# Attention and MLP on one core: the third group's values right behind its denominators, two turns a burst sooner, four second-MLP pieces in the first period

## The chip, the cores and the metric

The kernel runs on one core of one Trainium2 chip. The metric is the time of an execution in microseconds (us), in medians. Ratios are the mean time of one kernel's fast runs over the mean of the other's fast runs of the same rounds, so they are not quite the ratio of the medians quoted beside them. "Faster" or "slower" needs 2%, here 9 us; smaller differences are read from the ratio's 95% interval.

## The reference

```python
q, k, v: (8 batches, 12 heads, 448, 64);  g_q, g_k: (64,)
q_n, k_n = q / rms(q) * g_q, k / rms(k) * g_k
attn = softmax(q_n @ k_n.T / 8);  x = (attn @ v), heads side by side: (3584, 768)
h = x @ w_in                       # 768 x 2048
g = max(h, 0) + alpha * min(h, 0)
out = g @ w_out                    # 2048 x 768
```

## The kernel before

A batch's 12 heads are worked on in three groups of 4 heads, so there are 24 groups, numbered 0 to 23. A group has 7 score tiles. The program is a list of 66 bursts; a burst holds two or three score tiles and their exponentials, sometimes a group's denominators (`den`) or values (`attv`), and, from the end of batch 0 on, pieces of the MLP: up-projections (`up`, x times w_in, one of 16 tiles of the hidden layer) and second-MLP pieces (`down`, times w_out). Between a batch's last `attv` and the next batch's lies a period, whose bursts share out 16 `up` and some `down`.

The scheduling is by hand: every engine runs its instructions in the order in which this program emits them.

```python
    pss = ... "pss", bufs=2, PSUM      # score tiles, 2 banks each
    psa = ... "psa", bufs=1, PSUM      # one accumulator of 2 banks: den, attv, turns, spare
    psf = ... "psf", bufs=2, PSUM      # two of 1 bank: up, down, early turns, spin
    ...
    def square(y, nm):   # y >= 2: GpSimd
    def reduce(y, nm):   # VectorE: sums of squares
    def root(y):         # ScalarE: Ln, Exp
    def scale(y, nm):    # VectorE for q of groups 1 to 3, GpSimd for their k; then GpSimd for both
    def turn(y):         # TensorE transposes, VectorE writes qT and kT (k with its gain)
    ...
    # plan of the bursts
        if len(dens) > len(avs):
            avs[n] = len(avs)
        elif len(dens) < NG and last_in.get(len(dens), n) < n:
            dens[n] = len(dens)
    ...
    turn_at[2] = av_at[0] + 1
    for y in range(G, NG):
        early = y < G + 2
        n = turn_at[y - 1] if early else max(d for d in dens if d <= turn_at[y] - 2)
        at(n - (8 if early else 5), load_qk, y)
        for nm in "qk":
            (after if early else at)(n - 2, square, y, nm)
            if early:
                after(n, reduce, y, nm)
    ...
        roots[n + 1] = y
    ...
        tail = len(new) if b == B - 1 else 2 if odd or b == 0 else 1
    ...
    # burst of group 2's denominators (lead), and the next
        if lead and n in dens:
            den(dens[n]); log(dens[n]); invert(dens[n])
        elif lead:
            attv(avs[n])
```

With one accumulator, group 2's values can only start when ScalarE's logarithm has read the denominators. `spin` is a dummy matmul; the program puts spins where TensorE has nothing else to run.

Of the kernel before, what the change touches and what calls it, by code (L numbers as in the profile page):

```python
# [9 lines left out]
FP32 = mybir.dt.float32  # L10
# [11 lines left out]
def kernel(  # L22
# [14 lines left out]
    B, H, S, D = q.shape  # L37
# [4 lines left out]
    G = HH // 2  # L42
# [6 lines left out]
    TD = min(8, NG)  # L49
# [5 lines left out]
    pss = ctx.enter_context(tc.tile_pool(name="pss", bufs=2, space=bass.MemoryType.PSUM))  # L55
    psa = ctx.enter_context(tc.tile_pool(name="psa", bufs=1, space=bass.MemoryType.PSUM))
# [118 lines left out]
    def turn(y):  # L175

        if y >= TD:
            t = qkT[y, "k"].rearrange("p j g c -> p (j g c)")
            nc.vector.tensor_scalar(
                out=t, in0=t, scalar1=gain[:, 0:1], scalar2=None, op0=ALU.mult  # L180
            )
            return
        if y < G:
            ps = [psf.tile([128, 512], FP32, name="tps", tag="mm") for _ in "qk"]
        else:
            ps2 = psa.tile([128, 2, 512], FP32, name="tps2", tag="acc")
            ps = [ps2[:, 0], ps2[:, 1]]
        tps = [
            t[:, : S].bitcast(FP16).rearrange("p (j c) -> p j c", j=J) for t in ps
        ]  # L190
        for tp, nm in zip(tps, "qk"):
            for j in range(J):
                nc.tensor.transpose(  # L193
                    tp[:, j, :], qs[y, nm][:, j].rearrange("p h d -> p (h d)"), ident
                )
        for tp, nm in zip(tps, "qk"):
            t = att.tile([128, J, 2, 64], FP16, name=f"{nm}T", tag=f"{nm}T", bufs=4)
            o = t.rearrange("p j g c -> p j (g c)")
            if nm == "q" and y == 0:
                nc.scalar.copy(out=o, in_=tp)  # L200
            elif nm == "q":
                nc.vector.tensor_copy(out=o, in_=tp)
            else:
                nc.vector.tensor_scalar(  # L204
                    out=o, in0=tp, scalar1=gain[:, 0:1], scalar2=None, op0=ALU.mult
                )
            qkT[y, nm] = t
# [23 lines left out]
            scale=QK_SCALE, bias=expb[:, 0:1],  # L231
        )

    def over_keys(name, y, weights):
        acc = psa.tile([128, 2, 512], FP32, name=name, tag="acc")
        e = expT[y]
        for j in range(J):
            for g in range(2):
                for par in range(2):
                    nc.tensor.matmul(  # L240
                        out=acc[ds(64 * par, 64), g, :S],
                        lhsT=weights(g, par, j),
                        rhs=e[ds(64 * g, 64), j, par, :],
                        start=(j == 0),
                        stop=(j == J - 1),
                    )
        return acc
# [5 lines left out]
    def log(y):  # L253
        r = att.tile([128, 2, S], FP32, name="rden", tag="rden")
        nc.scalar.activation(out=r, in_=rden[y][:, :, :S], func=AF.Ln)  # L255
        rden[y] = r

    def invert(y):
        r = rden[y]
        nc.scalar.activation(out=r, in_=r, func=AF.Exp, scale=-1.0)  # L260

    def attv(y):
        b, i = divmod(y, G)
        vv = vt[b]
        av = over_keys("av", y, lambda g, par, j: vv[ds(64 * g, 64), 2 * i + par, j, :])
        if i == 0:
            xT[b] = att.tile([128, 2, G, S], FP16, name="xT", tag="xT")
        nc.vector.tensor_mul(  # L268
            out=xT[b][:, :, i, :], in0=av[:, :, :S], in1=rden[y]
        )  # L270
# [52 lines left out]
    def spin(count):  # L323

        if count:
            ps = psf.tile([128, 512], FP32, name="spin", tag="mm")
            for _ in range(count):
                nc.tensor.matmul(
                    out=ps[:, :S], lhsT=ident, rhs=idle, start=True, stop=True
                )  # L330
# [6 lines left out]
    while m < NG * J or len(avs) < NG:  # L337
        n = len(bursts)
        if len(dens) > len(avs):
            avs[n] = len(avs)  # L340
        elif len(dens) < NG and last_in.get(len(dens), n) < n:
            dens[n] = len(dens)
        three = n in dens and dens[n] >= G or n in avs and avs[n] >= G
        count = min(3 if three else 2, NG * J - m)
        bursts.append([divmod(m + c, J) for c in range(count)])
        for y, j in bursts[n]:
            first_in.setdefault(y, n)
            if j == J - 1:
                last_in[y] = n
        m += count  # L350
# [11 lines left out]
    turn_at = {  # L362
        y: max(n for n in range(first_in[y]) if n not in dens) for y in range(1, NG)
    }
    turn_at[2] = av_at[0] + 1
    turns = {n: y for y, n in turn_at.items()}
    jobs = {}
    for y in range(G, NG):

        early = y < G + 2  # L370
        n = turn_at[y - 1] if early else max(d for d in dens if d <= turn_at[y] - 2)
        at(n - (8 if early else 5), load_qk, y)
        for nm in "qk":
            (after if early else at)(n - 2, square, y, nm)
            if early:
                after(n, reduce, y, nm)
            else:
                jobs.setdefault(n, []).append((reduce, (y, nm)))
        roots[n + 1] = y
# [7 lines left out]
    for b in range(B):  # L387
        ups = [(UP, up, (b, ft)) for ft in range(NF)]
        odd = b % 2
        new = [  # L390
            (DOWN, down, (b - odd, t, oh))
            for t in (range(3, J) if odd else range(3)) for oh in range(2)
        ]
        tail = len(new) if b == B - 1 else 2 if odd or b == 0 else 1
        periods.append((ups, carry, new[:tail]))
        carry = new[tail:]

# [91 lines left out]
    for n in range(NB):  # L489
        for f, a in prep.get(n, ()):  # L490
            f(*a)
        tiles = bursts[n]

        lead = n in (den_at[G - 1], av_at[G - 1])
        if lead and n in dens:
            den(dens[n])
            log(dens[n])
            invert(dens[n])
        elif lead:
            attv(avs[n])  # L500
        for t in tiles[:2]:
            score(*t)
        plain = n not in dens and n not in avs
        wait = plain and gaps[n] and gaps[n][0][0] is up
        if lead and n in avs:
            spin(3)
        for t in tiles[:1] if wait else tiles[:2]:
            soft(*t)
        if n in dens and not lead:
            den(dens[n])  # L510
        if n in avs and not lead:
            attv(avs[n])
        for t in tiles[2:]:
            score(*t)
            soft(*t)
        late = []
        if wait:
            late = [(1, soft, t) for t in tiles[1:]]
        if n in roots:
            y = roots[n]  # L520
            root(y)
            for nm in "qk":
                scale(y, nm)
            if y >= TD:
                turn_dma(y)
        if n in dens and not lead:
            log(dens[n])
            if gaps[n] and gaps[n][0][0] is down:
                invert(dens[n])
            else:  # L530
                late = [(1, invert, (dens[n],))]
        done = 0

        spare_at, clock = [], 0.0
        for k, (f, a) in enumerate(gaps[n][:-1]):
            free = 2.3 if n in dens else 1.2 if n in avs else 0.1
            if clock >= free and not turns.get(n, TD) < TD and (
                not spare_at or k - spare_at[-1] > 2
            ):
                spare_at.append(k)  # L540
            clock += DOWN if f is down else UP
        for k, (f, a) in enumerate(gaps[n]):
            spare = k in spare_at
            if f is down:
                down(*a, jobs.pop(n, ()), spare)
            else:
                f(*a, spare)
                done += 1
                if late and done == late[0][0]:
                    for _, g, c in late:  # L550
                        g(*c)
                    late = []
            if n in turns and k == (
                0 if turns[n] >= TD else max(min(1, len(gaps[n]) - 2), 0)
            ):
                turn(turns[n])
        if not gaps[n] and n in turns:
            turn(turns[n])
        for _, g, c in late:
            g(*c)  # L560
        if n < den_at[G - 1] - 1 and plain and n not in turns:
            spin(4)
        elif lead and n in dens:
            spin(8)
        for f, a in jobs.pop(n, []) + post.get(n, []):
            f(*a)
    for k, (f, a) in enumerate(rest):
# [31 lines left out]
```

## Time and profile before

| | before |
|---|---|
| median of 3 runs | 449.81 us (449.42 to 450.79) |
| span of the profile | 449.1 us |
| TensorE, ScalarE, VectorE, GpSimd busy | 95%, 65%, 46%, 38% |
| first up-projection | 46.92 us |

The prediction below shows the lines and how they are read.

### The profile page before, as it was taken

The page shows a single profiled execution, that of the slowest core. Times are in us where ns is not written, and L with a number is a line of the kernel's source. Part 1 is how long each engine was busy: PE and PEld are TensorE (multiplying, and loading weights), DVE is VectorE, ACT ScalarE, POOL GpSimd, SP SyncE. Part 2 cuts the span into 40 slices and gives each one's busy share as a digit, 9 for nine tenths or more (in the row PEclk, how much of TensorE's full clock was granted, in tenths as well). Part 3 has the DMA queues.
Part 4 walks back from the last instruction along what each step waited for, and adds up shares of the span by engine and source line. Part 5 has one row for each costly group of instructions (what it writes and reads, how often), then busy time and mean ns, then how long its engine had stood idle before and what let it go on. Part 6 is the DMA issues. An engine that isn't in the chain of part 4 may idle for free.

```text
span 449.1 us, 9101 instructions
## 1 busy us (share of the span) xinstructions
PE 426.1 (95%) x3844; PEld 230.2 (51%) x3844; DVE 207.9 (46%) x297; ACT 290.9 (65%) x401; POOL 171.3 (38%) x125
## 2 busy tenths in 40 slices
PE   6877889889999999999999999999999999999996
PEld 2344444555545555545555545545555545555563
DVE  2656454735454545445454545444553343243421
ACT  4899788578776768578675868568675857222300
POOL 4769954660671460760671460760642000000000
PEclk9699999999999999999999999999999999999999
DMA  8999997295656651773567651782353401111122
GB/s 183 231 234 241 234 241 148 27 186 127 136 102 143 160 118 41 121 180 80 136 103 176 159 125 37 124 184 72 77 92 82 77 2 37 36 35 36 35 72 70
DMA packets 60009, 52.77 MB, mean 118 GB/s; under 512 B 32688, under 2 KB 56512, under 8 KB 59968
## 3 DMA queue, kind: packets, MB, share of 16 engines
q1 hardware_dynamic: 47424, 39.27, 37.3%
q0 software_dynamic: 11808, 11.81, 16.9%
q10 hardware_dynamic: 736, 1.11, 1.1%
q8 instruction: 30, 0.49, 0.5%
q14 instruction: 11, 0.09, 0.1%
HBM read 45.62 MB, written 11.01 MB: 126 GB/s over the span
## 4 chain that ended last, share of the span: by engine, by line
PE 82%; ACT 10%; DVE 4%; DMA 1%; issue 1%; POOL 0%; SPq 0%; ACTq 0%
PE op L301 32%; PE hT L284 19%; PE hTa L284 10%; PE sc L217 8%; ACT expT L229 5%; PE dn L240 5%; PE av L240 5%; PE opa L301 2%; DMA nat<-in_k_dram 1%; ACT ah L292 1%; ACT rden L260 1%; PE tps L193 1%; ACT rden L255 1%; DVE gT L293 1%; DVE ss L141 1%
## 5 line engine op out<-in xcount | busy, mean ns | idle before, releaser
L229 ACT ACTIVATE expT<-sc,expb 128x896 f16<-128x896 f32 x168 | 158.3, 1008 | 20.0 <-PE sc L217 19.7
L301 PE MATMUL op<-w_out_sb,gT 128*128 128x384 f16 x848 | 145.4, 326 | 0.0
L158 POOL TENSOR_TENSOR qs<-nat,rr 128x896 f16<-128x896 f32 x44 | 78.4, 1800 | 175.5 <-issue 138.1
L301 PEld LDWEIGHTS <-gT 128*128 128x128 f16 x896 | 84.6, 98 | 62.5 <-issue 9.1
L284 PE MATMUL hT<-xT,w_in_sb 128*128 128x448 f16 x534 | 112.7, 353 | 1.4 <-DVE gT L293 1.4
L284 PEld LDWEIGHTS <-w_in_sb 128*128 128x128 f16 x768 | 73.8, 98 | 71.5 <-issue 6.8
L292 ACT ACTIVATE ah<-hT,cols 128x448 f16<-128x448 f32 x89 | 56.5, 635 | 64.2 <-PE hT L284 64.1
L293 DVE TENSOR_TENSOR gT<-hT,ah 128x448 f16<-128x448 f32 x89 | 55.6, 625 | 64.8 <-ACT ah L292 64.8
L135 POOL TENSOR_TENSOR sq<-nat 128x896 f32<-128x896 f32 x44 | 73.1, 1683 | 1.5 <-DVE kT L204 1.4
L313 DVE COPY osb<-op 128x384 f32<-128x384 f32 x53 | 29.6, 558 | 93.6 <-PE op L301 93.6
L217 PE MATMUL sc<-qT,kT 64*64 64x448 f16 x672 | 53.8, 364 | 9.8 <-ACT expT L229 5.1
L141 DVE TENSOR_REDUCE ss<-sq 128x14 f32<-128x896 f32 x48 | 49.9, 1077 | 6.7 <-ACT sq L133 6.5
L284 PE MATMUL hTa<-xT,w_in_sb 128*128 128x448 f16 x234 | 50.6, 352 | 0.0
L292 ACT ACTIVATE ah<-hTa,cols 128x448 f16<-128x448 f32 x39 | 24.7, 635 | 39.6 <-PE hTa L284 39.6
L293 DVE TENSOR_TENSOR gT<-hTa,ah 128x448 f16<-128x448 f32 x39 | 24.4, 625 | 34.5 <-ACT ah L292 34.5
L217 PEld LDWEIGHTS <-kT 64*64 64x64 f16 x672 | 19.1, 105 | 40.0 <-issue 28.0
L240 PE MATMUL av<-expT,vt 64*64 64x448 f16 x672 | 36.0, 350 | 2.2 <-ACT rden L255 2.2
L240 PE MATMUL dn<-expT,ones 64*64 64x448 f16 x672 | 35.9, 349 | 0.2 <-DVE gT L293 0.2
L268 DVE TENSOR_TENSOR xT<-av,rden 128x896 f16<-128x896 f32 x24 | 26.2, 1091 | 21.3 <-PE av L240 20.2
L240 PEld LDWEIGHTS <-vt 64*64 64x64 f16 x672 | 20.6, 107 | 14.0 <-issue 3.7
L240 PEld LDWEIGHTS <-ones 64*64 64x64 f16 x672 | 20.6, 107 | 11.5 <-issue 0.6
L260 ACT ACTIVATE rden<-rden 128x896 f32<-128x896 f32 x24 | 22.9, 954 | 0.7
(37 smaller groups left out, 133.0 us busy)
## 6 DMA issues: line engine op xcount, KB each, us to landing
out_dram<-osb SPq DMA_DIRECT2D x54, 192.0 KB, 2.7
nat<-in_q_dram SPq DMA_DIRECT2D x46, 224.0 KB, 6.4
nat<-in_k_dram SPq DMA_DIRECT2D x46, 224.0 KB, 6.7
vt<-in_v_dram POOLq DMA_DIRECT2D x16, 336.0 KB, 8.3
w_in_sb<-in_moe_w_in_dram POOLq DMA_DIRECT2D x4, 768.0 KB, 13.2
w_out_sb<-in_moe_w_out_dram POOLq DMA_DIRECT2D x4, 768.0 KB, 16.8
nat<-in_q_dram ACTq DMA_DIRECT2D x2, 224.0 KB, 5.0
nat<-in_k_dram ACTq DMA_DIRECT2D x2, 224.0 KB, 6.2
```

The costliest lines, as they stand in the source:

```text
L135: nc.gpsimd.tensor_mul(out=sqf, in0=src, in1=src)
L141: nc.vector.tensor_reduce(out=ss_t[y][:, "qk".index(nm)].rearrange("p h j -> p (h j)").unsqueeze(2), in_=sqs[y, nm], axis=AXIS_X, op=ALU.add,)
L158: eng.tensor_mul(out=t.rearrange("p j h d -> p h j d"), in0=nat[y, nm], in1=rr_t[y][:, "qk".index(nm)].unsqueeze(3).broadcast_to((128, 2, ...
L217: nc.tensor.matmul(out=sc[ds(64 * g, 64), par, :S].rearrange("p (j c) -> p j c", j=J), lhsT=kT[ds(64 * par, 64), j, g, :], rhs=qT[ds(64 * ...
L229: nc.scalar.activation(out=expT[y][:, j], in_=scs[y, j][:, :, :S], func=AF.Exp, scale=QK_SCALE, bias=expb[:, 0:1],)
L240: nc.tensor.matmul(out=acc[ds(64 * par, 64), g, :S], lhsT=weights(g, par, j), rhs=e[ds(64 * g, 64), j, par, :], start=(j == 0), stop=(j == ...
L260: nc.scalar.activation(out=r, in_=r, func=AF.Exp, scale=-1.0)
L284: nc.tensor.matmul(out=hT[:, :S], lhsT=w_in_sb[:, c, ts(ft, 128)], rhs=x[:, c, :], start=(c == order[0]), stop=(c == order[-1]),)
L292: nc.scalar.activation(out=ah, in_=hT[:, :S], func=AF.Copy, scale=alpha_sb[:, ft : ft + 1])
L293: nc.vector.tensor_max(out=gT[:, ft, ds((b & 1) * S, S)], in0=hT[:, :S], in1=ah)
L301: nc.tensor.matmul(out=op[:, :OH], lhsT=gT[:, ft, ts(t, 128)], rhs=w_out_sb[:, ft, ds(oh * OH, OH)], start=(ft == 0), stop=(ft == NF - 1),)
L313: nc.vector.tensor_copy(out=o[:, ds(oh * OH, OH)], in_=op[:, :OH])
```

## The change

The intent, as I read it from the diff: let group 2's values run while ScalarE works on its denominators, by giving them a score tile instead of the accumulator; have the keys of groups 2 and 3 turned before the scores need them; and use the burst thus gained in period 0 for two more second-MLP pieces.

```diff
-    def over_keys(name, y, weights):
-        acc = psa.tile([128, 2, 512], FP32, name=name, tag="acc")
+    def over_keys(name, y, weights, spare=False):
+        pool, tag = (pss, "sc") if spare else (psa, "acc")
+        acc = pool.tile([128, 2, 512], FP32, name=name, tag=tag)
 ...
             dens[n] = len(dens)
+            if dens[n] == G - 1:
+                avs[n] = G - 1
 ...
-        if y < G:
+        if y <= G:                      # turn of group 3 in the single banks too
 ...
-    turn_at[2] = av_at[0] + 1
+    turn_at[2], turn_at[3] = av_at[0], av_at[1]
 ...
-        n = turn_at[y - 1] if early else max(...)
+        n = turn_at[y - 1] + (y == G) if early else max(...)
 ...
-        tail = len(new) if b == B - 1 else 2 if odd or b == 0 else 1
+        tail = len(new) if b == B - 1 else 4 if b == 0 else 2 if odd else 1
 ...
-        if lead and n in dens:
-            den(dens[n])
-            log(dens[n])
-            invert(dens[n])
-        elif lead:
-            attv(avs[n])
+        if lead:
+            den(dens[n])
+            attv(avs[n], True, (log, invert))
         for t in tiles[:2]:
             score(*t)
+            if lead and t == tiles[0]:
+                spin(6)
 ...                                     # spins and the place of a turn in a plain burst: cut
```

More of the change, by code (lines that the diff above doesn't have):

```diff
@@ L260, in invert, with attv @@
         nc.scalar.activation(out=r, in_=r, func=AF.Exp, scale=-1.0)
-    def attv(y):
+    def attv(y, spare=False, jobs=()):
         b, i = divmod(y, G)
         vv = vt[b]
-        av = over_keys("av", y, lambda g, par, j: vv[ds(64 * g, 64), 2 * i + par, j, :])
+        av = over_keys(
+            "av", y, lambda g, par, j: vv[ds(64 * g, 64), 2 * i + par, j, :], spare
+        )
+        for f in jobs:
+            f(y)
         if i == 0:
@@ L370 @@
         early = y < G + 2
-        n = turn_at[y - 1] if early else max(d for d in dens if d <= turn_at[y] - 2)
+        n = turn_at[y - 1] + (y == G) if early else max(d for d in dens if d <= turn_at[y] - 2)
         at(n - (8 if early else 5), load_qk, y)
@@ L492 @@
         tiles = bursts[n]
-        lead = n in (den_at[G - 1], av_at[G - 1])
-        if lead and n in dens:
+        lead = n == den_at[G - 1]
+        if lead:
             den(dens[n])
-            log(dens[n])
-            invert(dens[n])
-        elif lead:
-            attv(avs[n])
+            attv(avs[n], True, (log, invert))
         for t in tiles[:2]:
             score(*t)
-        plain = n not in dens and n not in avs
+            if lead and t == tiles[0]:
+                spin(6)
+        plain = lead or n not in dens and n not in avs
         wait = plain and gaps[n] and gaps[n][0][0] is up
-        if lead and n in avs:
-            spin(3)
         for t in tiles[:1] if wait else tiles[:2]:
@@ L553 @@
             if n in turns and k == (
-                0 if turns[n] >= TD else max(min(1, len(gaps[n]) - 2), 0)
+                0 if turns[n] >= TD or plain else max(min(1, len(gaps[n]) - 2), 0)
             ):
@@ L562 @@
             spin(4)
-        elif lead and n in dens:
-            spin(8)
         for f, a in jobs.pop(n, []) + post.get(n, []):
```

## The prediction

> **What bounds the kernel now.** I read the page's busy shares first, then its 40 slices, then a table of busy time by stretch, then the timeline of the first 90 us instruction by instruction.
>
> ```profile
> PE 426.1 (95%) x3844; PEld 230.2 (51%) x3844; DVE 207.9 (46%) x297; ACT 290.9 (65%) x401; POOL 171.3 (38%) x125
> ...
> PE   6877889889999999999999999999999999999996
> ...
> ACT  4899788578776768578675868568675857222300
> ```
>
> TensorE is the bound (95%), and its holes are in the first quarter. The stretches show how many (columns: length, then busy time of PE, PEld, DVE, ACT, POOL, then clock, DMA share, GB/s):
>
> ```profile
> 22.60:31.20 8.60, 5.82 (x98) 3.60 (x101) 4.32 (x6) 7.69 (x10) 6.29 (x5) 1.00 1.16 225
> 31.20:39.90 8.70, 5.64 (x102) 3.18 (x94) 5.07 (x7) 8.57 (x11) 7.55 (x6) 1.00 1.18 232
> 39.90:46.90 7.00, 6.36 (x87) 3.10 (x88) 5.05 (x5) 6.04 (x10) 6.98 (x5) 1.00 1.17 261
> ...
> 95.00:103.00 8.00, 8.00 (x58) 4.23 (x56) 4.00 (x7) 4.30 (x7) 6.61 (x4) 1.00 0.82 152
> ```
>
> From 22.6 to 46.9 us only batch 0's attention can run. ScalarE is nearly full there (7.69 of 8.60, 8.57 of 8.70): two 0.9 us exponentials a burst, roots, logarithms. TensorE waits, or fills with dummy matmuls. GpSimd is nearly full too, which matters below. After 95 us TensorE has no hole. So all that the change can win or lose is idle TensorE time before it meets the old schedule again.
>
> The lines around the third group:
>
> ```profile
> 27.65 3.31 POOL L135 TENSOR_TENSOR sq<-nat 128x896 f32<-128x896 f32 x2
> 30.91 1.71 POOL L116 DMA_DIRECT2D w_in_sb<-in_moe_w_in_dram  x2
> 33.77 2.54 POOL L158 TENSOR_TENSOR qs<-nat,rr 128x896 f16<-128x896 f32 x1 [1.15 <-issue]
> 36.28 6.59 POOL L135 TENSOR_TENSOR sq<-nat 128x896 f32<-128x896 f32 x4
> 37.59 0.96 PE L193 MATMUL tps<-ident,qs 128*128 128x128 f16 x14
> 43.48 1.52 PE L240 MATMUL av<-expT,vt 64*64 64x448 f16 x28
> 43.64 3.34 POOL L158 TENSOR_TENSOR qs<-nat,rr 128x896 f16<-128x896 f32 x2
> 45.13 1.09 DVE L268 TENSOR_TENSOR xT<-av,rden 128x896 f16<-128x896 f32 x1 [1.14 <-ACT expT L229]
> 46.34 0.74 PE L328 MATMUL spin<-idle,ident 128*128 128x448 f16 x3
> 46.92 2.43 PE L284 MATMUL hT<-xT,w_in_sb 128*128 128x448 f16 x12
> ```
>
> The first MLP matmul, which ends the thin stage, starts at 46.92, after the third group's xT (done 46.22) and two more score tiles that waited for exponentials. Note GpSimd's order: squares of group index 3 (27.65), weights, scaling of index 3's k (33.77), and only then the squares of index 4 (36.28).
>
> **What the Trainium skill says.** "PSUM — Partial Sum Buffer", Specifications: 8 banks of 2 KiB per partition. The pools take all 8 (two score tiles of 2, one accumulator of 2, two single ones), so values right behind denominators can only go into a score tile. The same page, "Engine vs sequencer instructions": ScalarE, VectorE and GpSimd queues are strict FIFO. The trace agrees: index 4's inputs, issued at 19.45 and 20.80, had landed some 9 us later, yet their squares ran at 36.28, behind the scaling. "SBUF — State Buffer", "Who interferes with whom": a DVE instruction with two SBUF inputs contends with a GpSimd one that reads SBUF. It agrees: the scaling takes 2.54 us beside VectorE's scaling and 1.67 (3.34 for two, at 43.64) otherwise. "TensorE: Matmul & The Clock Gate", Part 1: an idle window of about 3.4 us drops the clock. The clock here is 1.00 from 22.6 us on, with waits up to 1.1; no run so far shows a longer one.
>
> **The change part by part.** Groups are counted from 0, so the title's third and fourth group are indices 2 and 3. Steps that I use, all from the timeline: an exponential every 0.90 us (3.69 for four), a root 0.48, a logarithm 0.94, an inverse 0.85 (starts 33.06, 33.54, 34.48, 35.33), a score tile 0.2 when nothing holds it, 0.44 from its start to its exponential (30.83 to 31.27), denominators or values 1.32, an up-projection 1.13, 14 transposes 0.8, a pair of reductions 2.1.
>
> I compared the compiled order of both programs. From burst 28 on (140.6 us before) they are the same, as are the real matmuls in total, so the difference in time is the difference in when burst 28 starts. Dummies change little (23 to 26 in the loop).
>
> (1) Turn of index 2 in burst 5 instead of 6. VectorE's k write, which held scores at 30.83, ends near 29.8 instead of 30.78. ScalarE's hole of 0.88 at 30.39 shrinks to about 0.2. Logarithm of group 1: 32.8 instead of 33.54. Gain 0.7 us on ScalarE.
>
> (2) Turn of index 3 in burst 8 instead of 9. Its condition also moves the squares of index 4 to the end of burst 6. In the compiled GpSimd order they, and the last w_in load, now stand ahead of the scaling of index 3's k. So: squares of 3 end at 30.96; one weight issue 0.86, two squares 3.31, another issue 0.86: the scaling starts at 36.0 instead of 33.77, and with 1.67, plus about half of the 0.9 that sharing with VectorE costs, it ends near 38.1 instead of 36.31. The turn in burst 8 wants it at 35.5. TensorE runs in order, so it stands some 2.5 us there with the next scores behind it. ScalarE ends its two exponentials at 36.4 and waits to 38.9; before, that exponential ran at about 37.1. Then the root of index 4 waits for two reductions behind the late k write (about 39.3 + 2.1 = 41.4), another hole of 0.6.
>
> (3) Values behind denominators. Exponential of the group's last tile 41.9 to 42.8, next one to 43.7, logarithm 43.7, inverse 44.65 to 45.6, xT 45.6 to 46.7. The values (1.32 us) run at 42.9 to 44.3 beside ScalarE, instead of waiting for the logarithm: the wait of 0.37 and the serial 1.5 us are really gone. But xT ends near 46.7 because (2) ate it. First MLP matmul: 46.95, where 46.92 was. Two score tiles (0.2 each) are still owed. Without (2) the same chain would put it near 44.
>
> (4) Bursts 11 to 15. The reductions of index 5 now stand on VectorE behind three MLP writes (52 to 54), and the root that needs them stands on ScalarE ahead of the fourth `ah`. I get waits of 1.6 and 0.6 for the seventh and eighth up-projection, against 0.25 and 0.88 before: +1.1. ScalarE enters burst 14 later, so the wait of 0.60 at 63.45 becomes about 1.5: +0.95.
>
> (5) Two more second-MLP pieces (16 x 0.163 = 2.6 us each) in period 0. They replace up-projections in bursts 16 and 17, which carry a 0.63 `ah` each. ScalarE is eased, and the wait of 0.79 at 80.49 and smaller ones there go: -1.6. In return bursts 23 to 25 of period 1 hold 3, 3 and 2 up-projections with no second-MLP piece. In burst 24 ScalarE needs 2.85 + 1.9 + 3 x 0.64 = 6.7 where TensorE needs 5.5; over the three 16.75 against 15.4, and with the buffers' turns I get +1.75.
>
> Sum: 0.45 (start and owed scores) + 1.1 + 0.95 - 1.6 + 1.75 = +2.65 us. My chains by hand take each wait in full, so I shade it to +1.8.
>
> **The rivals.** (A) The change does what it intends: GpSimd isn't late, the first MLP matmul starts near 44, and most of the gain of 2 to 3 us, less owed scores, reaches the end: 447.5 to 449. For it: the serial wait is truly removed, and the author tuned around it. Against it: GpSimd is busy for 7.55 of 8.70 us there, and the order is fixed. (B) My chain in full: 452.5. (C) The first second-MLP piece comes earlier and waits for the last w_out chunk, which landed at 74.3 before (issued 56.44, 17.9 us later). By my count it is read near 79 and issued near 52, so there is no wait; should the piece come at 70, up to 4 us would be lost: 454. (D) TensorE's long wait drops the clock: one window at half rate costs under 2 us: 453.5. I expect about 2.5 us idle, so not quite.
>
> **Range and chances.** 449.8 + 1.8 = 451.6 us. The range 449.0 to 453.8 takes in part of A, all of B and most of D. Two per cent is 9 us; everything movable is in TensorE's idle 17 us of the first 95 (by the same table of stretches 46.9 less 35.05 busy up to 46.9, and 48.1 less 42.85 from there to 95), much of which no reordering can fill, so either side of 2% has 1 in 100.
>
> **What would show it.** Step 2: in the changed trace the 14 transposes of index 3 (the third such block) end near 38.5, the last one waiting for GpSimd's qs, with GpSimd's squares ahead; the longest ScalarE hole of the thin stage (2 us or more) follows. Step 3: the first hT at 46 to 48. If it is at 44 to 45, step 2 is wrong. Step 4: a wait over 1 us of an hT on gT near 55. Step 5: first op between 76 and 80 with no wait on a DMA, and new waits of hT on gT near 118 to 132. Burst 28 (the values after the ninth group's denominators and two op pieces) begins 1 to 3 us later than 141.1. If the time is under 449, step 2 or the period 1 term is wrong.

## The result, and the profile after

| | before | changed |
|---|---|---|
| median | 450.14 us (449.42 to 450.79, 4 runs) | 453.86 us (453.63 to 454.91, 4 runs) |
| ratio | | 1.0087, interval 1.0064 to 1.0111 |

The change costs 0.87%, nearly 4 us. The direction is as predicted, the size is not: 453.86 is just over the range's end of 453.8, and twice the +1.8.

**Where the two time axes are set level.** The first microseconds differ between executions of one and the same kernel: in the profile of before, TensorE waited 1.83 us for a small DMA at 9.00, in that of the changed kernel 0.30. Up to group 0's values the two programs are the same on TensorE. So I compare both traces from the start of these values: 25.87 us before, 24.61 in the changed kernel, and 1.26 us are added to a time of the changed kernel where it is set beside one of before ("on before's clock"; other runs likewise).

**The thin stage.** The page of the changed kernel, its row of granted clock, then stretches of its trace (columns as in the prediction):

```profile
PEclk9898999999999999999999999999999999999999
```

```profile
22.60:31.20 8.60, 7.28 (x118) 4.15 (x111) 5.39 (x6) 8.46 (x12) 7.35 (x5) 1.00 1.19 245
33.90:37.30 3.40, 0.61 (x11) 0.39 (x7) 3.38 (x3) 1.25 (x2) 3.38 (x3) 1.00 1.18 213
37.30:42.50 5.20, 5.09 (x51) 2.26 (x52) 2.67 (x3) 3.38 (x6) 4.88 (x4) 0.67 1.22 225
```

Up to 31 us all is well: ScalarE, which bounds the stage, is busy for 8.46 of 8.60 us, better than before. Then comes a stretch of 3.4 us in which TensorE works for 0.61 and ScalarE for 1.25, while VectorE and GpSimd are full. After it the clock is at 0.67 for 5 us. The timeline tells what VectorE and GpSimd do there:

```profile
30.54 3.32 POOL L135 TENSOR_TENSOR sq<-nat 128x896 f32<-128x896 f32 x2
31.61 4.14 DVE L158 TENSOR_TENSOR qs<-nat,rr 128x896 f16<-128x896 f32 x1 [0.79 <-ACT rr L153]
33.81 0.87 POOL L116 DMA_DIRECT2D w_in_sb<-in_moe_w_in_dram  x1
34.70 2.60 POOL L158 TENSOR_TENSOR qs<-nat,rr 128x896 f16<-128x896 f32 x1
35.81 0.56 PE L193 MATMUL tps<-ident,qs 128*128 128x128 f16 x7 [1.86 <-DVE qs L158]
37.35 0.90 PE L193 MATMUL tps<-ident,qs 128*128 128x128 f16 x7 [0.98 <-POOL qs L158]
38.82 1.90 ACT L229 ACTIVATE expT<-sc,expb 128x896 f16<-128x896 f32 x2 [3.66 <-PE sc L217]
46.64 2.44 PE L289 MATMUL hT<-xT,w_in_sb 128*128 128x448 f16 x12
```

The first line is group 4's squares on GpSimd, which the change put ahead of the scaling of group 3's k (34.70; 33.77 before, which is 2.19 us earlier once the axes are level). That was foreseen. The second line was not: VectorE's scaling of group 3's q, 1.09 us elsewhere, takes 4.14. It is entered at 31.61 and done at 35.75, so it is held until GpSimd is past both squares and the weights' issue. So the turn waits first for q (1.86), then for k (0.98), and ScalarE stands for 3.66 us with no scores. The scaling of k, which ends last (37.30), started when the prediction said (35.96 on before's clock, against 36.0); it takes 2.60 instead of 1.67, as it runs beside the held multiplication. From its end to the next exponential pass 1.52 us, while TensorE's granted clock is 0.50 (37.42 to 40.83). The first up-projection comes at 46.64, set to before's clock 47.90: 0.98 later than before. The score tile has a price too, though a small one: a score waits 0.68 us, at 46.33, until VectorE has made xT from the values in it.

**Period 0.** ScalarE and TensorE of the changed kernel, then the same moment in words:

```profile
51.87 2.07 DVE L141 TENSOR_REDUCE ss<-sq 128x14 f32<-128x896 f32 x2
53.98 0.32 ACT L152 ACTIVATE rr<-ss,epsb 128x28 f32<-128x28 f32 x1 [1.78 <-DVE ss L141]
54.46 0.62 ACT L297 ACTIVATE ah<-hT,cols 128x448 f16<-128x448 f32 x1
55.79 1.29 PE L289 MATMUL hT<-xT,w_in_sb 128*128 128x448 f16 x6 [1.14 <-DVE gT L298]
```

The reductions of group 5 end at 53.94, the root waits 1.78 us for them, the fourth `ah` waits behind the root, and TensorE waits 1.14 for the bank that this `ah` reads: step 4 of the prediction, in its order.

**Period 1.** Here the same stretch of both traces, first before, then the changed kernel:

```profile
103.00:139.00 36.00, 35.33 (x347) 19.13 (x347) 19.52 (x27) 28.81 (x39) 14.88 (x10) 1.00 0.63 131
```

```profile
103.00:139.00 36.00, 32.94 (x303) 16.81 (x306) 18.53 (x27) 28.19 (x40) 18.99 (x13) 1.00 0.53 110
```

TensorE is idle for 3.06 us of 36 instead of 0.67. Three waits make it up:

```profile
118.40 1.29 PE L289 MATMUL hT<-xT,w_in_sb 128*128 128x448 f16 x6 [0.67 <-DVE gT L298]
125.10 1.30 PE L289 MATMUL hT<-xT,w_in_sb 128*128 128x448 f16 x6 [1.01 <-DVE gT L298]
132.44 0.38 PE L217 MATMUL sc<-qT,kT 64*64 64x448 f16 x4 [1.34 <-DVE kT L179]
```

The first two are up-projections that wait for a bank whose `ah` and `gT` are late, in bursts 23 and 24, which now hold three up-projections each. The third is a score that waits for its key's gain, a VectorE multiplication (131.42, 0.97 us) that stands behind two reductions (2.07), the xT product (1.08) and a `gT`.

**The sum.** Each row is the shift of the changed kernel against before that arises in a stage, from group 0's values on. Where work moved into the stage it is taken off: 4 up-projections at 1.135 us before burst 14, 2 second-MLP pieces at 2.6 less these 4 up-projections in bursts 14 to 19, and the 2 pieces back in bursts 19 to 28.

| Stage, by its end | shift of the end | arises there |
|---|---|---|
| first up-projection | +0.98 | +0.98 |
| denominators of group 3 (burst 14) | +6.71 | +5.73 - 4.54 = +1.19 |
| denominators of group 5 (burst 19) | +6.58 | -0.13 - 0.66 = -0.79 |
| values of group 8 (burst 28) | +4.31 | -2.27 + 5.20 = +2.93 |

After burst 28 both programs are the same, and the shift stays. The 4.31 us of these two profiles is a little more than the times show (+0.87% of 450, 3.9).

### The profile page after: what moved, and what is told of

Same layout as the page of the kernel before. It is cut to its first block, busy times and chain, and to the rows that moved or that the text cites. A ratio compares the mean times of both kernels' runs of the same rounds, so it can differ in the third digit from the quotient of the medians.

```text
span 452.2 us, 9104 instructions
## 1 busy us (share of the span) xinstructions
PE 429.0 (95%) x3847; PEld 230.8 (51%) x3847; DVE 210.9 (47%) x297; ACT 290.4 (64%) x401; POOL 171.2 (38%) x125
## 3 DMA queue, kind: packets, MB, share of 16 engines
q10 hardware_dynamic: 736, 1.11, 1.0%
## 4 chain that ended last, share of the span: by engine, by line
PE 79%; ACT 8%; DVE 4%; POOL 3%; issue 3%; DMA 2%; SPq 0%; ACTq 0%; POOLq 0%
PE op L306 31%; PE hT L289 18%; PE hTa L289 10%; PE sc L217 6%; PE dn L241 5%; PE av L241 5%; ACT expT L229 4%; ACT ah L297 2%; POOL sq L135 2%; PE opa L306 2%; DMA nat<-in_q_dram 2%; DVE gT L298 1%; DVE ss L141 1%; PE tps L193 1%; POOL qs L158 1%
```

## The experiments

Fourteen kernels ran, with five rounds each beside the kernel before; all gave correct results. They ran in four batches, each on a chip of its own, so runs of different batches are compared by their ratios. The columns "first up" and "burst 28" are shifts against before in the profiles, from group 0's values on, as above.

| Run | median us | ratio to before (95%) | first up | burst 28 |
|---|---|---|---|---|
| the change | 453.86 | 1.0087 (1.0064 to 1.0111) | +0.98 | +4.31 |
| turns alone | 451.80 | 1.0042 (1.0028 to 1.0056) | +1.91 | +2.05 |
| values alone | 450.24 | 1.0008 (0.9992 to 1.0023) | -1.63 | +0.73 |
| four pieces alone | 451.24 | 1.0026 (1.0011 to 1.0042) | 0.00 | +1.39 |
| three pieces alone | 450.54 | 1.0010 (0.9992 to 1.0027) | +0.73 | +1.41 |
| change, clock held | 453.70 | 1.0084 (1.0071 to 1.0098) | +0.66 | +4.00 |
| change, three pieces | 452.64 | 1.0056 (1.0043 to 1.0070) | +0.95 | +2.60 |
| change, two pieces | 452.97 | 1.0062 (1.0048 to 1.0075) | +0.66 | +3.01 |
| change, squares back | 451.13 | 1.0019 (1.0000 to 1.0038) | -2.97 | +0.38 |
| squares back, two pieces | 453.45 | 1.0064 (1.0047 to 1.0082) | -2.98 | +2.37 |
| squares back, values loaded early | 450.26 | 1.0009 (0.9995 to 1.0022) | -2.98 | +0.37 |
| and reductions first ("repaired") | 448.64 | 0.9970 (0.9958 to 0.9982) | -2.98 | -1.15 |
| repaired, three pieces | 447.19 | 0.9935 (0.9923 to 0.9947) | -2.98 | -2.59 |
| repaired, two pieces | 447.87 | 0.9954 (0.9940 to 0.9968) | -2.98 | -2.07 |
| repaired, three, values serial | 448.66 | 0.9969 (0.9955 to 0.9982) | -1.73 | -1.26 |

The theory after the two traces: (1) the squares of group 4 ahead of group 3's scaling cost the thin stage; (2) the second-MLP pieces taken from period 1 leave TensorE waiting there. The rival: (3) the values in a score tile hold up the scores whatever GpSimd does. Later came (4) to (6): a late load, late reductions, the clock.

### The squares back

```diff
-        n = turn_at[y - 1] + (y == G) if early else ...
+        n = turn_at[y - 1] + 1 if early else ...
```

> The changed kernel with the squares, reductions and root of group index 4 one burst later, where the kernel before had them; all else of the change stays. Theory 1 (the squares ahead of the scaling of index 3's k on GpSimd cost the thin stage): the scaling of k starts 3 us or more before 34.7 + the start-up's shift, TensorE's wait at the third turn is under 1 us, the clock stays at 1.00 there, the first up-projection comes near 44.5 instead of 46.6, and the time is 2 to 3 us under the changed kernel's 453.9, so 451 to 452. Theory 2 alone (only the bursts after 46 us, by the moved second-MLP pieces, cost): the time stays within 0.7 us of 453.9. Rival 3 (the values in a score tile hold up the scores whatever GpSimd does): the time stays at 453 or more though the turn no longer waits.

Measured: 451.13 us, as theory 1 has it. The edit moves the reductions and the root of group 4 (and its loads) with the squares. The turn, in the timeline of this run:

```profile
31.43 1.09 DVE L158 TENSOR_TENSOR qs<-nat,rr 128x896 f16<-128x896 f32 x1 [0.79 <-ACT rr L153]
31.54 2.53 POOL L158 TENSOR_TENSOR qs<-nat,rr 128x896 f16<-128x896 f32 x1 [0.35 <-issue]
34.04 6.59 POOL L135 TENSOR_TENSOR sq<-nat 128x896 f32<-128x896 f32 x4
42.51 2.44 PE L289 MATMUL hT<-xT,w_in_sb 128*128 128x448 f16 x12
```

VectorE's multiplication takes 1.09 us again. (It takes 4.14 or 4.15 in all five traces with the squares ahead of the scaling, 1.09 in the others.) The scaling of k starts 2.98 us sooner than in the changed kernel, with the axes level, and the first up-projection 3.95 sooner. One line of the diff, a `(y == G)`, costs that. Theories 2 alone and 3 fall for the thin stage. In the two profiles nearly all of it reaches burst 28 (+4.31 against +0.38); by the times it is 0.0068 of 450, 3.1 us. This profile is of the quickest of the run's six executions, 1.3 us under their median. A wait that wasn't there before could be what differs from execution to execution; that isn't shown:

```profile
64.33 1.51 PE L241 MATMUL av<-expT,vt 64*64 64x448 f16 x26 [1.30 <-DMA vt<-in_v_dram]
```

Batch 1's values now come too late. Their load was issued at 45.44 and took 14.6 and 18.1 us for its two halves (10.5 and 12.1 us for the same load in the kernel before).

### Two pieces, in the changed kernel and with the squares back

```diff
-        tail = ... 4 if b == 0 else 2 if odd else 1
+        tail = ... 2 if odd or b == 0 else 1
```

> The changed kernel with two second-MLP pieces in period 0 as before, not four. Theory 2 (period 1 is left with up-projections alone and TensorE waits there for ScalarE and VectorE, 3.0 us in bursts 23 to 26): those waits go and about 1 us comes back as a cost in bursts 17 and 18, so the time falls by 1.2 to 2.5 us to 451.4 to 452.7. Theory 1 alone: within 0.7 us of 453.9.

Measured: 452.97 us, 0.9 below the change; a little less than theory 2 asked for.

> Both edits at once: squares of index 4 back, two second-MLP pieces in period 0. Theories 1 and 2 together: the gains add up to 3.5 to 5 us, so 449 to 450.4, level with the kernel before (450.1) or a little faster. If only one is true the time equals that one's run. Rival 3: 452 or more.

Measured: 453.45 us, a miss by 3 us: the two gains don't add, together they are worse than the squares alone. That is in the range that rival 3 was given, but the first up-projection still comes 2.98 sooner than before, so the loss arises after the thin stage. Most of it is in the trace:

```profile
63.99 2.61 PE L241 MATMUL av<-expT,vt 64*64 64x448 f16 x26 [2.65 <-DMA vt<-in_v_dram]
66.03 0.94 PE L217 MATMUL sc<-qT,kT 64*64 64x448 f16 x4
```

With two pieces the up-projections are dealt out more slowly, the values of group 3 come sooner still (61.00 instead of 62.68), and wait 2.65 us for the load; after that four score matmuls take 0.94 us instead of 0.38, at a granted clock of 0.50. This profile is the quickest of its six runs (451.89 us, up to 454.40), so in others the wait was probably longer; only one trace is at hand. A later run supports this reading: the early load and the earlier reductions together gain 1.10% with two pieces, and 0.49% with four, where the wait is shorter.

### Four and three pieces in the kernel before

```diff
-        tail = ... 2 if odd or b == 0 else 1
+        tail = ... 4 if b == 0 else 2 if odd else 1     # the second run: 3
```

> The kernel before with four second-MLP pieces in period 0 and nothing else. Theory 2: period 1's waits appear without any change in the thin stage; 1.2 to 2.5 us over before, so 451.3 to 452.6. If the pieces do harm only together with the other parts: within 0.7 us of 450.1.

> The kernel before with three second-MLP pieces in period 0. Theory 2: the gain of the third piece does not hang on the rest; no wait of 1.3 us in burst 26 and the ones of bursts 17 to 19 smaller: 448.7 to 449.6. Rival: three are worth something only with the short thin stage: 449.9 or more.

Measured: 451.24 us with four, 0.26% over before, so they cost without any of the rest, and the wait of 1.34 us for the key's gain is there (at 129.70). With three 450.54 us, a miss: I expected a gain and there is none, the interval holds 1, though the wait for the key's gain is gone. Its profile has its first up-projection 0.73 late, though the program is that of before up to there. The trace tells why:

```profile
39.10 2.83 PE L240 MATMUL dn<-expT,ones 64*64 64x448 f16 x28
41.97 0.92 ACT L255 ACTIVATE rden<-dn 128x896 f32<-128x896 f32 x1 [0.62 <-PE dn L240]
```

The granted clock was 0.50 from 38.95 to 42.37, so group 2's denominators took 2.83 us instead of 1.49 and the logarithm waited for them. In the trace with four pieces the clock was 1.00 there. So this one profile is not a clean one; how often the clock fell in the runs without a trace isn't known.

### The values of batch 1 loaded early, and the reductions first

```diff
-        at(av_at[G * b] - 4, load_v, b)
+        at(av_at[G * b] - (7 if b == 1 else 4), load_v, b)
```

> The run with the squares back, plus the load of batch 1's values issued three bursts sooner, ahead of the second weight matrix. Theory 4 (once the thin stage is short, the values of batch 1 land too late, since the DMA engines are busy throughout, and that wait of 1.3 us and more, which differs from run to run, hides a part of the gain): no wait of the values' matmuls on that load, runs closer together, and 1.0 to 2 us under the 451.1 of the run with the squares back: 449 to 450. If the wait is hidden by others anyway: 451 again. If the weights now come late instead: a wait of the first down-projection on a DMA.

Measured: the load lands after 10.9 and 12.4 us and no matmul waits for it. The time is 450.26 us, 0.10% below the run without it by the ratios, with overlapping intervals; and in the profiles burst 28 shifts from +0.38 to +0.37. Here other waits take the place of the 1.30 us: the same stage now has one of 0.79 for an exponential and one of 1.12 for xT (0.44 before the edit). So theory 4 missed its size in this kernel. The times do lie closer together (449.91 to 451.63, against 449.82 to 452.56).

```diff
             attv(avs[n], True, (log, invert))
+            for f, a in jobs.pop(n, []):      # reductions of group 5 ahead of the MLP pieces
+                f(*a)
```

> The run with the early values, plus the two reductions of index 5 ahead of burst 11's up-projections on VectorE. Theory 5 (step 4 of the prediction: these reductions behind three MLP writes hold the root, the fourth ah and so the seventh up-projection): the wait of 1.1 us of an up-projection on gT some 9 us after the first one goes, and the time falls by 0.5 to 1.2 us against the run with the early values. Rival: the wait moves to the scores or to the turn of index 4, and the time stays.

Measured: 448.64 us, 0.39% less than the run before it. The wait of 1.14 us of an up-projection is gone from the list of waits and burst 28 shifts by 1.52, all of it before burst 14. The gain is above the range that I wrote down (0.5 to 1.2), the step is right.

### Two, three, four pieces in the repaired kernel, and three in the changed one

> As the run before it, with three second-MLP pieces in period 0, not four. Theory 2 (period 1 with two old pieces only is short of TensorE work without ScalarE work): waits of 3 us in bursts 23 to 26 shrink to about 1, bursts 17 and 18 give back at most 0.5: 1 to 2 us faster than with four, so 447 to 448.5, under the kernel before by 2 us or so. Rival: the piece only moves the wait between the periods and the time stays within 0.5.

> The repaired kernel (squares back, values early, reductions first) with two second-MLP pieces in period 0, as the kernel before has; so far four gave 448.6 and three 447.2. Theory 2 in its plain form (each piece taken from period 1 costs): two are at least as good as three, 446.0 to 447.3. Theory 2b (the best number is the one that fits: with nine bursts in period 0 two leave TensorE short there): two are 0.7 us or more worse than three, 447.9 to 449.5.

> The changed kernel with three second-MLP pieces in period 0; four gave 453.9 and two 453.0. Plain theory 2: between the two, 453.2 to 453.7. Theory 2b: three are the best, 451.8 to 452.6, as in the repaired kernel.

Measured: four 448.64, three 447.19, two 447.87 in the repaired kernel; four 453.86, three 452.64, two 452.97 in the changed one. Four is worse than three in both: in the repaired kernel the intervals don't touch, in the changed one they overlap by 0.0006. Two and three can't be told apart: their intervals overlap in both kernels (and 447.87 lies between the two ranges written down), so "a number that fits", which I wrote down as theory 2b, is not settled against "each piece costs".

Where three gains over four can be read in the shifts from burst 19 to burst 28. In the repaired kernel four pieces go from +1.11 to -1.15, which is -2.26, and with two pieces of 2.6 us taken out of the stage this is 2.94 us of waits. Three go from -1.26 to -2.59, and with one piece taken out that is 1.27 us. With two, -2.07 and -2.07, none. The same sums give 2.93, 1.28 and 0 in the changed kernel, and 2.94, 1.27 and 0 in the kernel before. So in period 1 each piece that is taken away costs, whatever the thin stage does. Before burst 19 the third piece saves 1.79 us (repaired) and 1.68 (changed) by the same reckoning, a little more than its 1.27 in period 1; that is why two and three end so near each other.

### The clock held

```diff
         for f in jobs:
             f(y)
+        if y == 1:
+            spin(8)                            # ahead of group 3's turn
```

> The changed kernel with 8 dummy matmuls ahead of the third turn, where TensorE stands 1.9 us and then 1.0, and after which its granted clock was 0.67 for 5 us. Theory 6 (the clock's drop is a part of the loss): the clock stays over 0.9 there, the scores, dummies and denominators after the turn take 2 us less between them, and the time falls by 0.5 to 1.5 us from 453.9. Rival: ScalarE, not TensorE, ends these bursts, so the clock is restored and the time stays within 0.4 us.

Measured: 453.70 us against 453.86, the same. The stretch that had clock 0.67 in the changed kernel is at 1.00 here:

```profile
37.30:42.50 5.20, 3.75 (x51) 2.03 (x52) 3.48 (x5) 2.89 (x5) 5.18 (x5) 1.00 1.23 213
```

The first up-projection comes 0.32 us sooner and burst 28 by 0.31 in the profiles, and the times can't show that little. So the low clock is at most a small part of this loss, as the rival in the expectation said. That the dummies held the clock is not shown: in the run with the turns alone, next, the clock stayed at 1.00 without them.

### The turns alone and the values alone

The first is the kernel before with the lines on `turn_at`, `y <= G` and `(y == G)` of the change. The second is the changed kernel with `turn_at`, `(y == G)` and the number of pieces put back; it keeps `y <= G` and the spins of the change.

> The kernel before with the two turns a burst sooner alone, with the squares of index 4 where the change puts them; values behind the logarithm and two second-MLP pieces as before. Theory 1: the same blocked scaling on VectorE (4 us instead of 1.1) and late scaling of k on GpSimd; the first up-projection comes 1 to 2.5 us later than before, 451 to 452.5. Rival 3: the turns alone gain, 449.5 or less.

> The kernel before with the third group's values right behind its denominators alone: turns, squares and second-MLP pieces as before. Theory 1: without the squares' move GpSimd is on time, so the first up-projection comes 1.0 to 1.6 us sooner than before (45.3 to 45.9 on its clock); 0.4 us of scores stay owed and the reductions of index 5 behind the MLP writes cost up to 1.1, so 449.3 to 450.4, level with before. Rival 3 (the values in the score tile do the harm): 451 or more.

Measured: the turns alone cost 0.42%, and their timeline has the same held multiplication:

```profile
31.65 4.15 DVE L158 TENSOR_TENSOR qs<-nat,rr 128x896 f16<-128x896 f32 x1 [0.79 <-ACT rr L153]
35.86 0.56 PE L193 MATMUL tps<-ident,qs 128*128 128x128 f16 x7 [1.86 <-DVE qs L158]
37.40 0.56 PE L193 MATMUL tps<-ident,qs 128*128 128x128 f16 x7 [0.98 <-POOL qs L158]
38.33 1.91 ACT L229 ACTIVATE expT<-sc,expb 128x896 f16<-128x896 f32 x2 [3.12 <-PE sc L217]
```

The waits of TensorE are those of the changed kernel, 1.86 and 0.98 us, but here the granted clock stays at 1.00:

```profile
33.94:37.34 3.40, 0.62 (x11) 0.39 (x7) 3.39 (x3) 1.26 (x2) 3.38 (x3) 1.00 1.18 217
37.34:42.54 5.20, 4.14 (x59) 2.27 (x60) 4.54 (x5) 3.71 (x6) 4.46 (x4) 1.00 1.22 224
```

From the end of k's scaling (37.35) to the exponential pass 0.98 us, where the changed kernel needs 1.52: some 0.5 us of ScalarE's wait there is the low clock's.

The values alone bring the first up-projection forward by 1.63 us and the time stays with before (1.0008, the interval holds 1). Rival 3 falls. The three parts alone cost 0.42, 0.08 and 0.26%, in sum 0.76, and the whole change 0.87: within the intervals they add.

### The values serial again in the best kernel

From the kernel before, with both turns sooner, the squares where they were, the early load and three pieces; group 2's values behind the logarithm as ever.

> The best run so far (three pieces) with the third group's values behind the logarithm, as in the kernel before, so the earlier turns, early values load and three pieces without the values' move. If the values' move is worth what step 3 says (the serial wait less two owed score tiles): the first up-projection 0.7 to 1.5 us later and the time 0.3 to 1.2 us over 447.2. Rival: ScalarE's chain sets the end either way and the time is within 0.3 of 447.2.

Measured: 448.66 us against 447.19, so the values' move, which is worth nothing by itself, is worth 0.34% here, where the reductions are in neither kernel behind MLP writes and the rest is on time. That is 1.5 us, a little above the range written down (0.3 to 1.2). The first up-projection is 1.25 us later without it, as expected.

**A version that beats both.** The repaired kernel with three pieces ran at 447.19 us, 0.9935 of before (0.9923 to 0.9947) and 6.7 us under the change.

## Why the prediction was right or wrong

- **What bounds it**: right. Everything was decided before burst 28, and the programs run level after it.
- **Step 1** (logarithm of group 1 at 32.8): right, 31.48 on its own clock, 32.74 on before's.
- **Step 2** (the squares stand ahead; TensorE stands at the third turn): the mechanism is right, and undoing it alone gave 3.1 us by the times. The size is too small. I wrote that "sharing with VectorE" costs GpSimd "about half of the 0.9"; it cost all of it, 0.93, because VectorE's scaling, held for 3.05 us, ended at 35.75, after GpSimd's had started (34.70). So k was ready at 38.56 on before's clock, against "near 38.1". The exponentials, expected at 38.9, came at 38.82 on their own clock, 40.08 on before's; of these 1.18 us some 0.5 each are k's delay and the low clock.
- **Step 3** (first up-projection at 46.95): mis-sized for those reasons. The term +0.05 measured +0.98. Its counter-claim, "without (2) the same chain would put it near 44", was right: 42.51 in the run with the squares back, 43.95 on before's clock (its group 0 values start at 24.43). That the values "can only go into a score tile" is too strong: the two single banks are as large together, and no up-projection needs them before; that wasn't tried.
- **Step 4** (waits in bursts 11 to 15): with the owed scores +1.5 predicted up to burst 14, +1.19 measured. For bursts 14 to 19 steps 4 and 5 together said +0.95 - 1.6 = -0.65; measured -0.79. Right as a sum. Undoing the late reductions alone was worth 1.52, where I had 1.1.
- **Step 5** (period 1): the term +1.75 measured +2.93. The two waits on `gT` were foreseen; the score that waits 1.34 us for its key's gain was not, since I counted ScalarE's work there and not the order on VectorE.
- **The last step failed outright**: the chain by hand gave +2.65, and I shaded it to +1.8, because "my chains by hand take each wait in full". No line of the profile asked for that. The waits were there in full, and two of them larger. By the terms, 0.98 + 1.19 - 0.79 + 2.93 = 4.31 stands against 0.05 + 1.5 - 0.65 + 1.75 = 2.65.
- **The rivals**: A (the change does what it intends) was wrong for the change; without its slip the first up-projection did come near 44, but the time was still 451.13, not 447.5 to 449. B, the chain in full, 452.5, had the right mechanism and fell 1.4 short. C (a late w_out chunk) didn't happen: the first `op` started at 76.69 and waited for no DMA. D (the clock) happened, against my expectation, and cost 0.3 us in the profiles and nothing that could be timed. Its figure, 453.5, is the nearest of all, by luck: the terms above make up the loss, not the clock. I expected about 2.5 us idle and held that for too short. But the trace of before already had a fall to 0.50, from 11.20 to 18.03, after waits of 1.83 and 0.64.

What stays open: whether two or three pieces are the better number; how long the wait for batch 1's values was in the runs that have no trace; and what makes the clock fall in one execution and not in another with the same waits.

## What to carry to other kernels

When a transposition or a load is moved ahead in a hand-made schedule, look at what else takes its place from the same variable: here the squares of the next group moved with the turn and stood ahead of the work that the turn needs, which cost 3.1 us, where the best version gains 2.9 over the kernel before. Read the order of each engine's queue around the moved instruction before believing the saved wait. And where a chain worked out from measured durations gives a number, record that number: a discount "for caution" needs a line of the profile as much as any other term.

## What the Trainium skill lacked or had wrong

- "SBUF — State Buffer", "Who interferes with whom": it has the contention of a two-input VectorE instruction with a GpSimd one that reads SBUF, but not that the wait can outlast the GpSimd instruction in flight. Here a multiplication of 1.09 us took 4.14 (4.14 or 4.15 in four other runs): it was held for 3.05 us, past the end of two GpSimd squares that followed each other (30.54 to 33.86).
- "TensorE: Matmul & The Clock Gate", Part 1: it has the clock fall after an idle window of about 3.4 us, but not how much work a window may hold and still count as idle. Here the granted clock fell to 0.50 after 3.41 us in which TensorE worked for 0.64 (changed kernel, at 37.42), and even for 1.90, with no wait over 0.99 (three pieces alone, at 38.95); with 0.62 of 3.40 (turns alone) it stayed at 1.00. So the waits alone don't tell whether it falls.
